# Weight pairs converted as one 512-wide tile, three step tables in place of two, in a fused attention and mixture-of-experts kernel

## The chip, the cores and the metric

The kernel runs on one core of a Trainium2 chip. The metric is the device time of one execution in microseconds (us), from the kernel's start to its end; lower is better. The profiled execution is one more execution, seen by the hardware profiler. Engines are named as the profile names them: PE is TensorE (PEld its weight loads), DVE is VectorE, ACT is ScalarE, POOL is GpSimd, SP is SyncE, whose queue issues most of the DMAs.

## The reference

Three layers follow one another. The two weight matrices of the middle layer arrive as 64-bit floats; everything else is 32-bit.

```
# 1: attention, 4 batches x 8 heads, 576 positions, 64 wide, top 32 of each row
scores = scale * q @ k.T
kth = np.partition(scores, -32, axis=-1)[..., -32:-31]
scores = np.where(scores >= kth, scores, -1e9)
x = softmax(scores) @ v                       # -> 2304 tokens x 512

# 2: dense layer, w_in 512 x 2048 and w_out 2048 x 512 (float64)
h = x @ w_in
x = (h * np.clip(h + 3.0, 0.0, 6.0) / 6.0) @ w_out

# 3: one of 8 experts for each token
logits = normed(x) @ normed(expert_emb).T / tau
e = argmax(logits);  gate = softmax(logits)[e]
out[token] = gate * (relu(x[token] @ w1[e]) @ w2[e])
```

## The kernel before, in words

**Units and steps.** The attention is cut into 72 units; a unit is 128 query rows of two heads. The kernel walks through 76 steps of a software pipeline. In step `i` the scores of unit `i` are computed, the top 32 of unit `i-1` are picked, unit `i-2` is masked, unit `i-3` goes through the exponential and is scaled, and unit `i-4` is transposed and multiplied by V. The picking is done on DVE: `pairs` (lines 409 to 413) sorts the 576 scores of each row into two halves, and `select` (lines 428 and 431, called `pick0` to `pick3`) takes eight maxima at a time. Line 411 runs once for each unit, so the distance between two of its rows is the length of a step.

**The dense layer beside it.** From step 12 on, each step also works on one of 72 items of the dense layer (nine groups of 256 tokens, eight slices of the hidden width each): `s10` and `s11` are the first product on PE (line 568), `gate` and `large` are ACT's, `swish` is DVE's, `small` is POOL's, and `s20` and `s21` are the second product (line 603) for the item of the step before. The steps in `PAUSE` take no item. A finished group is written to `y_dram` (`out_y`) and its tokens are scored against the experts (`route`, then `choose`, `rank` and `place`, taken one at a time by `aside`).

**The weights.** In the first steps the float64 weights are converted, in 32 pairs of pieces, each piece 128 x 256. `w_load` brings the two words of each number, one piece a tile. DVE shifts the exponent and the upper mantissa bits of the high word into place with two operations per piece, both reading two tiles in SBUF (`w_one`, line 234, and `w_two`, line 238). The 29 low bits are then treated in one of two ways: three pieces of four are rounded on ACT (`w_round`, line 246) and added on POOL (`w_add`, line 251), one of four is merged by a third DVE operation (line 241). The result is split into a high part on ACT (`w_hi`, line 259) and a low part on POOL (`w_low`, line 263), and the low part is stored to DRAM (`w_store`). Steps 0 to 4 convert one pair each (`RAMP`), steps 5 to 18 up to two.

**The order.** Inside the loop the order of instructions is written out by hand: the strings `FIRST` (steps 0 to 20, `WORDS`) and `THEN` list the parts of a step, and every engine and every DMA queue takes its instructions in that order.

**The end.** After the loop a scheduler orders the code by priorities. The last group of the dense layer (tokens of groups 16 and 17) is a special case before: its second product, the routing of its tokens (`finals`), the first half-layer of expert 0 (`stage1(0, ...)`) and the splitting of that expert's weights are interleaved by hand (lines 992 to 1026), and the weights of the second expert are asked for ahead of them. Then the eight experts follow.

Of the kernel before, what the change touches and what calls it, by code (L numbers as in the profile page):

```python
# [54 lines left out]
def fused_kernel(tc: tile.TileContext, *args):  # L55
# [35 lines left out]
def layers(tc: tile.TileContext, qt, kt, v, w_in, w_out, embt, tau, w1, w2, out, y_dram, g_dram, x_dram, tbl, lo_dram, flag, pools, consts):  # L91
# [4 lines left out]
    m1, sm, fs, ps_a = pools[1:]  # L96
# [26 lines left out]
    stg = st.enter_context(tc.tile_pool(name="stg", bufs=5))  # L123
# [24 lines left out]
    def embed(part):  # L148
# [6 lines left out]
        elif part == 1:  # L155
            onesf = mp.tile([128, 128], F32, tag="ug", name="onesf", bufs=1)
            nc.vector.memset(onesf, 1.0)
            sq = fs.tile([128, 4, E], F32, tag="gts", name="sq")
            nc.vector.tensor_tensor(sq, emb["et"], emb["et"], op=ALU.mult)
# [3 lines left out]
        elif part == 2:  # L163
# [30 lines left out]
    wpieces = []  # L194
    for q in range(8):
        c = slice(256 * q, 256 * q + 256)
        for k in range(4):
            wpieces.append((w_in[128 * k:128 * k + 128, c], (vh[:, k - k % 2:k - k % 2 + 2, c], lo_dram[0][q][:, 256 * (k - k % 2):256 * (k - k % 2) + 512])))
        for k in range(2):
            for c in (slice(0, 256), slice(256, 512)):  # L200
                wpieces.append((w_out[128 * (2 * q + k):128 * (2 * q + k) + 128, c], (wh[:, 2 * q + k, :], lo_dram[1][q][:, 512 * k:512 * k + 512])))
    ent_ = {}
    cnt, stored = [0], [0]
# [23 lines left out]
    def w_one(n):  # L227
        e = ent_[n]
        e["both"] = mp.tile([128, DM], F32, tag="wf", name="wf", bufs=3)
        for o, (raw, single, _) in enumerate(e["raws"]):  # L230
            if single:
                nc.vector.tensor_copy(e["both"][:, 256 * o:256 * o + 256], raw)
# [937 lines left out]
```

## Time and profile before

| | us |
|---|---|
| median of three runs | 1165.76 |
| lowest and highest of them | 1165.2 and 1168.55 |
| the profiled execution, its own time | 1164.9 |
| its span, first to last instruction | 1163.2 |
| busy: PE, DVE, ACT, POOL | 1008.5, 818.5, 732.6, 646.4 |
| end of the conversion, start of line 411 in unit 18 | 241.9 |

The busy figures are for the whole span. Over the first 240 us DVE is busy nearly all the time and PE about half of it or less; from there on PE is busy nearly all the time. So the two stretches are read apart. An engine's rows overlap slightly (an instruction's row starts about 0.08 us before the one ahead of it on DVE has ended), so a sum over a step is taken from start to start.

### The profile page before, as it was taken

The numbers are of one execution on the slowest core, as the hardware profiler recorded it, in microseconds if no ns is written. First come the engines' busy times: TensorE is split into PE (matmuls) and PEld (weight loads), VectorE is DVE, ScalarE is ACT, GpSimd is POOL, SyncE is SP. The second block draws the span as 40 slices with busy tenths as digits, with TensorE's granted clock in tenths as the row PEclk, the third lists the DMA queues.
The fourth block names the chain that finished last, engine by engine and source line by source line (L and its number), as shares of the span: only waits on it lengthen the run. The fifth ranks groups of instructions, "written<-read, shape, count | busy, mean of one in ns | idle before, by whom it ended". The sixth has DMA issues, their size and how long they took to land. (4 is left out here: it accounts for less than half of the span.)

```text
span 1163.2 us, 21146 instructions
## 1 busy us (share of the span) xinstructions
PE 1008.5 (87%) x7200; PEld 892.1 (77%) x7200; DVE 818.5 (70%) x2429; ACT 732.6 (63%) x1486; POOL 646.4 (56%) x833
## 2 busy tenths in 40 slices
PE   2455576789999979999979998999989999999994
PEld 1344465679998869998868997889978788888884
DVE  4999999999788968788968789922142534444440
ACT  4676776878778868778868778743334444444540
POOL 5676776777666867666867666653231442213210
PEclk9966577889999989999989999999999999999998
DMA  6444455665443446443446244356765463344440
GB/s 179 146 137 138 164 167 174 185 199 204 123 123 116 134 144 194 123 123 118 136 121 213 82 146 128 110 128 177 235 214 208 117 221 122 128 175 148 173 175 20
DMA packets 93014, 176.45 MB, mean 152 GB/s; under 512 B 21135, under 2 KB 38690, under 8 KB 92895
## 3 DMA queue, kind: packets, MB, share of 16 engines
q1 hardware_dynamic: 88255, 164.90, 45.2%
q0 software_dynamic: 4640, 10.10, 2.6%
q8 instruction: 59, 0.97, 0.4%
q14 instruction: 60, 0.49, 0.1%
HBM read 151.15 MB, written 19.71 MB: 147 GB/s over the span
## 5 line engine op out<-in xcount | busy, mean ns | idle before, releaser
L446 POOL TENSOR_TENSOR s<-s,z 128x576 f32<-128x576 f32 x144 | 189.8, 1323 | 70.2 <-ACT z L442 69.5
L568 PE MATMUL bank_h<-xh,vh 128*128 128x256 f32 x576 | 177.0, 307 | 0.8 <-DVE u L580 0.8
L568 PE MATMUL bank_h<-xh,lo 128*128 128x256 f32 x576 | 167.7, 291 | 3.7 <-DMA lo<-lo_dram 3.7
L568 PE MATMUL bank_h<-xl,vh 128*128 128x256 f32 x576 | 167.7, 291 | 2.8 <-DVE xl L524 2.8
L428 DVE MAX8 A<-left 128x8 f32<-128x288 f32 (+1 forms) x288 | 159.7, 595 | 0.0
L397 PE MATMUL ps_sc<-kst,qh 128*128 128x288 f32 x256 | 90.8, 367 | 71.6 <-DVE left L413 35.9
L587 POOL TENSOR_TENSOR gl<-u,gh 128x512 fp32r<-128x512 f32 x72 | 93.2, 1295 | 102.8 <-ACT gh L584 88.8
L484 ACT COPY pt<-bank_t 128x384 f32<-128x384 f32 x216 | 100.4, 475 | 59.1 <-PE bank_t L479 58.9
L479 PE MATMUL bank_t<-ident,s 128*128 128x128 f32 x648 | 108.2, 294 | 28.0 <-ACT pt L484 16.7
L397 PEld LDWEIGHTS ps_sc<-kst,qh 128*128 128x128 f32 x256 | 55.7, 218 | 88.4 <-issue 73.6
L400 ACT COPY s<-ps_sc 128x576 f32<-128x576 f32 x144 | 91.5, 635 | 41.8 <-PE ps_sc L397 38.4
L568 PEld LDWEIGHTS bank_h<-xh,lo 128*128 128x128 f32 x576 | 114.2, 198 | 4.3 <-DMA lo<-lo_dram 4.3
L568 PEld LDWEIGHTS bank_h<-xl,vh 128*128 128x128 f32 x576 | 114.3, 198 | 3.6 <-DVE xl L524 3.1
L580 DVE SCALAR_TENSOR_TENSOR u<-u,bank_h 128x512 f32<-128x512 f32 x72 | 49.2, 684 | 95.6 <-ACT u L576 95.3
L603 PE MATMUL y<-wh,gh 128*128 128x512 f32 x288 | 116.3, 404 | 0.0
L807 DVE TENSOR_TENSOR l<-a,h 128x1024 fp32r<-128x1024 f32 x64 | 78.0, 1243 | 54.2 <-ACT h L806 51.5
L479 PEld LDWEIGHTS bank_t<-ident,s 128*128 128x128 f32 x648 | 82.3, 150 | 44.0 <-ACT pt L484 20.1
L568 PEld LDWEIGHTS bank_h<-xh,vh 128*128 128x128 f32 x576 | 114.2, 198 | 1.6 <-DVE u L580 1.0
L603 PE MATMUL y<-wh,gl 128*128 128x512 f32 x288 | 113.0, 397 | 2.0 <-POOL gl L587 2.0
L603 PE MATMUL y<-lo,gh 128*128 128x512 f32 x288 | 113.9, 396 | 0.2 <-DMA lo<-lo_dram 0.2
L442 ACT ACTIVATE z<-s,nb 128x576 bf16<-128x576 f32 x144 | 111.7, 780 | 0.8 <-POOL nb L436 0.7
L452 ACT ACTIVATE s<-s,nb 128x576 f32<-128x576 f32 x144 | 112.1, 778 | 0.0
(240 smaller groups left out, 2778.9 us busy)
## 6 DMA issues: line engine op xcount, KB each, us to landing
lo<-lo_dram SPq DMA_DIRECT2D x144, 512.0 KB, 4.2
a<-in_moe_w_dram SPq DMA_DIRECT2D x64, 512.0 KB, 7.4
qraw<-in_q_dram SPq DMA_DIRECT2D x64, 128.0 KB, 3.0
w<-in_moe_w_in_dram SPq DMA_DIRECT2D x32, 256.0 KB, 3.4
lo_dram<-wf SPq DMA_DIRECT2D x32, 256.0 KB, 2.4
w<-in_moe_w_out_dram SPq DMA_DIRECT2D x32, 256.0 KB, 3.0
vt<-in_v_dram SPq DMA_DIRECT2D x16, 320.0 KB, 4.5
kraw<-in_k_dram SPq DMA_DIRECT2D x32, 144.0 KB, 4.3
```

The source lines that it names most:

```text
L397: nc.tensor.matmul(ps[:, n, :HS], t, kk[:, HS * g:HS * g + HS], start=(o == 0), stop=(o == len(parts) - 1))
L400: nc.scalar.copy(sbuf[i % NS][:, :, HS * g:HS * g + HS], ps_[i][:, :, :HS])
L428: nc.vector.max(A[:, n, 8 * r:8 * r + 8], src[:, n, :w])
L442: nc.scalar.activation(zb_[n], tile_of(i, n), AF.Relu, bias=sel[i][1][:, n, 1:2], scale=-BIG)
L446: nc.gpsimd.tensor_tensor(s, s, zb_[n], op=ALU.subtract)
L452: nc.scalar.activation(s, s, AF.Exp, bias=sel[i][1][:, n, 0:1], scale=SCALE, accum_out=sums[i][:, n:n + 1])
L479: nc.tensor.transpose(pp[:, 128 * k:128 * k + 128], e[:, 128 * (3 * c + k):128 * (3 * c + k) + 128], ident)
L484: nc.scalar.copy(pts[i][:, 3 * c:3 * c + 3, :].rearrange("p k n -> p (k n)"), tb_.pop((i, c))[:, :384])
L568: nc.tensor.matmul(ph[:, a, :], w, x[:, k, :], start=(k == 0 and n == 0), stop=(k == 3 and n == 2))
L587: nc.gpsimd.tensor_tensor(state[q][1], state.pop((q, "u")).rearrange("p (a n) -> p a n", a=2), state[q][0].bitcast(F32), op=ALU.subtract)
L603: nc.tensor.matmul(state["y"][o], x[:, a, c], w, start=(f == 0 and n == 0), stop=(f == 15 and n == 2))
L807: nc.vector.tensor_tensor(lo, x, hi.bitcast(F32), op=ALU.subtract)
```

## The change

Conversion: a pair is loaded by one DMA into one tile of 512 numbers, three such tiles in place of five of 256. The first bit operation becomes a `tensor_scalar` (one tile and two constants), the second stays a `scalar_tensor_tensor`; both work on 512 numbers at once. Every pair is rounded on ACT and added on POOL; the third DVE operation is no longer reached. The tables: `FIRST` now holds for steps 0 to 11, the new `MID` for steps 12 to 20, and `THEN` has another order. The preparation of the expert embedding is cut into five parts and its square moves to ACT. At the end, the special case for the last group is gone: the last group goes through the same loop as the others, and the weights of the second expert are asked for later.

```diff
-RAMP, WORDS = 5, 21
-FIRST = ("turn0 lows ship hi0 expo0 low0 hi1 s10 keep0 load_k expo1 turn1 bend0 one0 guard pick0 store0 score0 low1 two0 mask0 pick1 "
-         "turn2 inverse s11 pick2 round1 bend1 keep1 take0 keep2 load_q mask1 s20 score1 round0 gate one1 scale two1 values swish "
-         "take1 large aside add0 store1 pick3 pairs load0 add1 xh load1 s21 small bounds xl prep need_v")
-THEN = ("pick0 turn0 turn1 expo0 keep0 s10 expo1 lows ship turn2 pick1 pick2 s11 keep1 keep2 guard bend0 score0 gate take0 load_k "
-        "values mask0 score1 inverse swish scale pick3 bend1 xh load_q take1 prep need_v mask1 bounds aside large s20 xl pairs "
-        "s21 small place")
+RAMP, MOES, WORDS = 5, 12, 21
+FIRST = ("hi0 turn0 bend0 keep0 turn1 pick0 lows ship turn2 bend1 keep1 keep2 expo0 expo1 pick1 one0 round1 s10 hi1 s20 s21 score0 "
+         "low0 load_k values take0 load_q two0 mask0 guard round0 inverse s11 store0 pick2 pick3 mask1 gate aside low1 xh score1 "
+         "scale swish take1 large prep one1 two1 add0 bounds small add1 xl load0 load1 pairs store1 need_v")
+MID = ("lows s10 round0 expo0 hi0 turn0 turn1 one0 expo1 s11 gate two0 s20 pick0 low0 pick1 guard s21 bend0 ship keep0 score0 "
+       "load_k store0 keep1 turn2 add0 hi1 swish one1 take0 mask0 keep2 load_q inverse score1 large values round1 two1 take1 "
+       "pick2 aside bend1 load0 scale xh pick3 low1 small add1 mask1 need_v pairs xl prep load1 store1 bounds")
+THEN = ("lows turn0 pick0 expo0 keep0 turn1 expo1 s10 s11 ship bend0 turn2 score0 keep1 pick1 guard gate take0 keep2 inverse "
+        "mask0 swish scale large aside bend1 pick2 load_k s20 pick3 score1 take1 s21 values small prep mask1 pairs place xh "
+        "bounds load_q xl need_v")
@@
-    stg = st.enter_context(tc.tile_pool(name="stg", bufs=5))
+    stg = st.enter_context(tc.tile_pool(name="stg", bufs=3))
@@ def embed(part):
-            sq = fs.tile([128, 4, E], F32, tag="gts", name="sq")
-            nc.vector.tensor_tensor(sq, emb["et"], emb["et"], op=ALU.mult)
+            emb["sq"] = fs.tile([128, 4, E], F32, tag="gts", name="sq")
+            nc.scalar.activation(emb["sq"], emb["et"], AF.Square)
+        elif part == 2:
+            onesf, sq = emb["ones"], emb["sq"]
@@ def w_one(n):
-            nc.vector.scalar_tensor_tensor(t, raw[:, :, 1], 3, raw[:, :, 1], op0=ALU.logical_shift_left, op1=ALU.bitwise_xor)
+        nc.vector.tensor_scalar(t, raw[:, :, 1], 3, 0x3FFFFFFF, op0=ALU.logical_shift_left, op1=ALU.bitwise_and)
@@ def w_two(n):
-            nc.vector.scalar_tensor_tensor(t, t, 0x3FFFFFFF, raw[:, :, 1], op0=ALU.bitwise_and, op1=ALU.bitwise_xor)
-            if not rounded:
-                nc.vector.scalar_tensor_tensor(t, raw[:, :, 0], 29, t, op0=ALU.logical_shift_right, op1=ALU.bitwise_or)
+        nc.vector.scalar_tensor_tensor(t, raw[:, :, 1], -0x40000000, t, op0=ALU.bitwise_and, op1=ALU.bitwise_or)
@@ def w_load(n):
-                raw = stg.tile([128, 256, 2], I32, tag="st", name="w64")
+            raw = stg.tile([128, 512, 2], I32, tag="st", name="w64")
-            raws.append((raw, single, cnt[0] % 4 != 3))
+        ent_[n] = dict(dst=dst, raw=raw, single=single, rounded=True)
@@ def out_y(o):
-            final = gs[o] >= NG - 2
-            if final:
-                finals.append((t, gs[o]))
-            else:
-                route(t, gs[o])
+            route(t, gs[o])
@@
-        while moe or side:
+        while moe or last or side:
@@
-        with tc.manual_schedule():
-            for o in range(2):
-                last[6](last[0], o)
...
-            load1(1)
...
-            stage1(0, 0, 256, (4,))
-            split2(0, range(5, 8), lambda f: stage1(0, 0, 256, (f,)))
+        with tc.high_priority(offset=500):
+            stage1(0, 0, 256)
+        split2(0)
@@
-                if r:
-                    load1(then)
+                load1(then)
                 load2(then)
```

## Rows read from the trace of the kernel before

**Rows 1.** Busy time in three stretches; columns: stretch, length, PE, PEld, DVE, ACT, POOL, PEclk.

```profile
81.60:94.30 12.70, 7.14 (x37) 5.67 (x37) 12.67 (x38) 9.12 (x21) 9.26 (x12) 0.50 0.40 137
158.20:241.90 83.70, 59.32 (x412) 51.85 (x413) 81.84 (x221) 63.59 (x134) 60.70 (x71) 0.81 0.59 183
241.90:745.00 503.10, 480.85 (x3938) 432.89 (x3937) 430.92 (x1503) 392.46 (x846) 358.93 (x503) 0.97 0.46 140
```

**Rows 2.** Timeline of DVE, line 411, units 0, 4, 11 and 18.

```profile
16.54 0.75 DVE L411 TENSOR_TENSOR left<-ps_sc,s 128x576 f32<-128x576 f32 x1
...
57.37 0.75 DVE L411 TENSOR_TENSOR left<-ps_sc,s 128x576 f32<-128x576 f32 x1
...
144.90 0.75 DVE L411 TENSOR_TENSOR left<-ps_sc,s 128x576 f32<-128x576 f32 x1
...
241.89 0.75 DVE L411 TENSOR_TENSOR left<-ps_sc,s 128x576 f32<-128x576 f32 x1
```

**Rows 3.** Timeline of DVE in one step, its conversions and what follows them.

```profile
88.13 0.51 DVE L428 MAX8 A<-top 128x8 f32<-128x144 f32 x2
...
90.74 0.75 DVE L234 SCALAR_TENSOR_TENSOR wf<-w 128x256 int32<-128x256 int32 x2
91.41 0.75 DVE L238 SCALAR_TENSOR_TENSOR wf<-wf,w 128x256 int32<-128x256 int32 x2
92.08 1.41 DVE L428 MAX8 A<-left 128x8 f32<-128x576 f32 x2
...
95.85 0.75 DVE L234 SCALAR_TENSOR_TENSOR wf<-w 128x256 int32<-128x256 int32 x2
96.52 0.51 DVE L428 MAX8 A<-top 128x8 f32<-128x144 f32 x2
...
97.50 1.94 DVE L238 SCALAR_TENSOR_TENSOR wf<-wf,w 128x256 int32<-128x256 int32 x2
99.36 1.50 DVE L241 SCALAR_TENSOR_TENSOR wf<-w,wf 128x256 int32<-128x256 int32 x1
100.79 0.51 DVE L428 MAX8 A<-top 128x8 f32<-128x144 f32 x2
```

**Rows 4.** Timeline of POOL at the same time; brackets: idle before, and its releaser.

```profile
91.96 1.49 POOL L251 TENSOR_TENSOR wf<-wf,w 128x256 int32<-128x256 int32 x2 [3.15 <-issue]
...
93.87 0.73 POOL L381 TENSOR_TENSOR ql<-qraw,qh 128x256 fp32r<-128x256 f32 x1
94.56 1.27 POOL L263 TENSOR_TENSOR wf<-wf,vh 128x512 fp32r<-128x512 f32 x1
...
97.70 2.88 POOL L446 TENSOR_TENSOR s<-s,z 128x576 f32<-128x576 f32 x2
```

**Rows 5.** Groups over the whole span: count | busy us, mean ns of one | idle before.

```profile
L580 DVE SCALAR_TENSOR_TENSOR u<-u,bank_h 128x512 f32<-128x512 f32 x72 | 49.2, 684 | 95.6 <-ACT u L576 95.3
L246 ACT ACTIVATE w<-w 128x256 int32<-128x256 uint32 x48 | 19.7, 442 | 1.8 <-DMA w<-in_moe_w_in_dram 1.7
```

**Rows 6.** Waits of PE, 158 to 242 us: total, times, longest.

```profile
PE bank_a L162 <- DVE sq L159: 9.3, 1, 9.3
```

**Rows 7.** Waits of PE, 242 to 745 us: total, times, longest.

```profile
PE bank_t L479 <- ACT pt L484: 14.5, 11, 2.9
```

**Rows 8.** Timeline of ACT near 410 us, where a new batch's keys arrive.

```profile
410.00 0.67 ACT L322 CAST kst<-kraw 128x576 fp32r<-128x576 f32 x1 [2.51 <-DMA kraw<-in_k_dram]
```

**Rows 9.** Timeline of PE and POOL around the end of the dense layer.

```profile
886.13 0.39 PE L603 MATMUL y<-wh,gl 128*128 128x512 f32 x1
887.20 0.66 PE L1008 MATMUL pxt<-ident,ysl 128*128 128x128 f32 x4 [0.68 <-ACT ysl L614]
...
899.42 0.98 POOL L699 DMA_INDIRECT tbl<-ids,rows  x1 [0.30 <-issue]
```

**Rows 10.** Busy time by stretch around and after it; columns as in rows 1.

```profile
886.00:915.00 29.00, 25.26 (x172) 22.34 (x171) 13.31 (x51) 13.83 (x26) 5.92 (x8) 0.97 0.54 154
915.00:1130.00 215.00, 211.72 (x1229) 185.20 (x1228) 101.83 (x133) 98.99 (x153) 60.52 (x59) 1.00 0.46 162
```

More of the change, by code (lines that the diff above doesn't have):

```diff
@@ L209, in w_load @@
     def w_load(n):
-        raws = []
-        for src, dst in (wpieces[2 * n], wpieces[2 * n + 1]):
-            single = src.dtype == F32
-            if single:
-                raw = stg.tile([128, 256], F32, tag="st", name="w32")
-                nc.sync.dma_start(out=raw, in_=src)
-            else:
-                raw = stg.tile([128, 256, 2], I32, tag="st", name="w64")
-                nc.sync.dma_start(out=raw, in_=src.bitcast(I32).rearrange("p (n two) -> p n two", two=2))
-                cnt[0] += 1
-            raws.append((raw, single, cnt[0] % 4 != 3))
@@ L221, in w_load @@
-        ent_[n] = dict(dst=wpieces[2 * n][1], raws=raws)
-    def words_of(e):
-        return [(raw, e["both"][:, 256 * o:256 * o + 256].bitcast(I32), rounded)
-                for o, (raw, single, rounded) in enumerate(e["raws"]) if not single]
+        src, dst = wpairs[n]
+        single = src.dtype == F32
+        if single:
+            raw = stg.tile([128, 2, 256], F32, tag="st", name="w32")
+            nc.sync.dma_start(out=raw, in_=src)
+        else:
+            raw = stg.tile([128, 512, 2], I32, tag="st", name="w64")
+            nc.sync.dma_start(out=raw.rearrange("p (a n) two -> p a n two", a=2), in_=src.bitcast(I32).rearrange("p a (n two) -> p a n two", two=2))
@@ L243, in w_round @@
     def w_round(n):
-        for raw, single, rounded in ent_[n]["raws"]:
-            if rounded and not single:
-                nc.scalar.activation(raw[:, :, 0], raw[:, :, 0].bitcast(U32), AF.Copy, scale=2.0 ** -29)
+        e = ent_[n]
+        if e["rounded"] and not e["single"]:
+            raw = e["raw"]
+            nc.scalar.activation(raw[:, :, 0], raw[:, :, 0].bitcast(U32), AF.Copy, scale=2.0 ** -29)
     def w_add(n):
-        for raw, t, rounded in words_of(ent_[n]):
-            if rounded:
-                nc.gpsimd.tensor_tensor(t, t, raw[:, :, 0], op=ALU.add)
+        e = ent_[n]
@@ L253, in parts_of @@
+        if e["rounded"] and not e["single"]:
+            nc.gpsimd.tensor_tensor(e["words"], e["words"], e["raw"][:, :, 0], op=ALU.add)
     def parts_of(e):
@@ L779, in finish_counts, with load_ids @@
             nc.vector.tensor_copy(flag[:, 1:2], vf)
-    def expert(r):
+    def load_ids(r, b0, b1):
         if r not in evs:
@@ L844, in ahead @@
         load2(0)
-        expert(1)
     def step(i, last):
@@ L939, in layers, with split2 @@
                 finish_rest()
-        assert "w1" in late and done_groups[0] == NG - 2
+        if "w1" not in late:
+            at.close()
+            ahead()
+        assert done_groups[0] == NG and "order" in late
+        st.close()
+        hp = mb.enter_context(tc.tile_pool(name="hp", bufs=1))
+        tk = mb.enter_context(tc.tile_pool(name="tk", bufs=1))
+        wb = mb.enter_context(tc.tile_pool(name="wb", bufs=1))
+        gp = mb.enter_context(tc.tile_pool(name="gp", bufs=3))
+        px = mb.enter_context(tc.tile_pool(name="px", bufs=2, space=PSUM))
+        po_ = mb.enter_context(tc.tile_pool(name="po_", bufs=3, space=PSUM))
         hs = {}
-        def split2(r, then=(), f=None):
-            then = deque(then)
+        def split2(r):
             a2 = ws2[r]
@@ L948, in split2, with stage1 @@
                 split(h2[:, k:k + 2, :], l2[:, k:k + 2, :], a2[:, k:k + 2, :])
-                if then:
-                    f(then.popleft())
             ws2[r] = (h2, l2)
-        def stage1(r, c0, c1, fs_=range(8)):
+        def stage1(r, c0, c1):
             xh_, xl_ = tok[r]
@@ L958, in stage1 @@
             hh, hl = hs[r]
-            for f in fs_:
+            for f in range(8):
                 ph = late["ph"].tile([128, 512], F32, tag="ph", name="ph2")[:, :c1 - c0]
```

84 lines of the change are left out of this document (27 added, 57 removed).

## The prediction

> **What bounds the kernel now.** I read busy time by stretch first, then the length of a step from line 411, then DVE and POOL side by side within one step, and last the waits of PE.
>
> In the early stretch DVE is busy for 12.67 of 12.70 us, ACT for 9.12, POOL for 9.26 and PE for 7.14 [rows 1]. DVE sets the step there. From 241.9 us on it is PE, busy for 480.9 of 503.1 us [rows 1], and so it stays through the experts, 211.7 of 215 us [rows 10]. What PE has to do after 241.9 us is nearly the same work in both kernels, so a microsecond won before that point should arrive at the end undiminished, as long as nothing behind it grows.
>
> Line 411 stands at 16.54, 57.37, 144.90 and 241.89 us for units 0, 4, 11 and 18 [rows 2]. The steps between are thus 40.83/4 = 10.21 us with one pair, 87.53/7 = 12.50 us with two pairs, and 96.99/7 = 13.86 us with two pairs and, mostly, an item of the dense layer beside them.
>
> Now the inside of a step of 12.66 us, 88.13 to 100.79 [rows 3]. The conversions take 90.74 to 92.08 (four operations, 1.34 us), 95.85 to 96.52 (two, 0.67 us) and 97.50 to 100.79 (three, 3.29 us): 5.30 us. What remains, the selection and small things, is 7.36 us. Undisturbed, one operation takes 1.34/4 = 0.335 us from start to start, so nine would take 3.02 us. The other 2.28 us are lost in the last group: the second operation there and the one behind it, each reading two tiles in SBUF, are held while POOL runs its two L446 back to back from 97.70 to 100.58 [rows 3, 4]. So DVE is not only full, it is also standing in line behind POOL.
>
> **The conversion.** *DVE.* Nine operations on 256 numbers become four on 512. The nearest row for one on 512 is L580, 684 ns [rows 5]; with the 0.08 us overlap between neighbours that is 0.60 us from start to start. Four cost 2.40 us, and DVE's own work in a step goes from 7.36 + 3.02 = 10.38 to 9.76 us. The first operation is now a `tensor_scalar`, which the trace does not show on such tiles. I bound it by 0.335 us (the price of half the numbers) and 0.60 us, and take 0.60, because L580 has the same shape; at the lower end DVE's work is 9.23 us.
>
> By the Trainium skill (VectorE: DVE Perf Modes, section "The perf-mode tier table") a 32-bit `tensor_scalar` from SBUF to SBUF runs at twice the rate of a two-tensor operation, which would put the price near the lower end. No row here shows such an operation.
>
> *POOL.* Two adds of 256 numbers take 1.49 us, so 0.745 each; from 256 to 512 numbers POOL's subtractions go from 0.73 to 1.27 us [rows 4], so an add of 512 costs about 0.745 x 1.27/0.73 = 1.30 us. Three adds in a step (0.745 x 2 + about 0.9 for one that is held) become two, 2.6 in place of 2.4 us: POOL goes from 9.26 to about 9.45 us. *ACT.* Three roundings at 0.44 us [rows 5] become two of twice the size, between 0.44 and 0.88 us each, so ACT moves by -0.4 to +0.4 us from 9.12: no bound.
>
> *Who stands in line now.* If DVE's second operations and POOL's work exclude each other, as the held pair shows, the two need 9.45 + 2 x 0.60 = 10.65 us a step. DVE alone needs 9.76, which leaves 0.9 us for waits. I take **10.6 us**. The lower end is 9.76 us, no wait at all; it would need POOL to be idle just then, as it is today before the first adds (3.15 us, [rows 4]). The upper end is that both second operations wait as long as the two held ones do today, 2.28 us together: 12.04 us.
>
> Stretch by stretch. Units 4 to 11: 7 x (12.50 - 10.6) = **13.3 us** (3.2 to 19.2). Units 11 to 18: today they stand 1.36 us above the others; I leave that, since the dense layer's ACT, DVE and POOL work is the same, so 11.96 us, 7 x 1.9 = **13.3 us** (3.2 to 22.8). The upper end there holds one thing more: PE waits 9.3 us for the square of the expert embedding, which sits at the end of a DVE step [rows 6], and the change moves it to ACT and puts a step between. Units 0 to 4: one pair costs 1.2 in place of 1.5 us and there is half the waiting; but new keys are cast on ACT there too. From 10.21 to 9.5 us: **2.8 us** (0 to 4.8). Together 29.4 us.
>
> *Fewer tiles, larger loads.* With three tiles for two pairs in work, the first load of the next step finds a free tile, the second waits until POOL has added the first pair, and on SP the store of the low part and the next `ship` stand behind it. In my reading of the new tables that add ends about 2 us ahead of the step's end and the second pair is wanted 4 to 5 us into the next step. I cost it at nothing; the cover is those 6 us, and if a load took longer, DVE would wait for the difference, once a step.
>
> **The order in `THEN`.** Of the 22.2 us for which PE is idle from 241.9 to 745 us, 14.5 us are 11 waits of transposes for ACT's copy `keep` [rows 7], the longest where a batch's new keys are late and hold ACT for 2.51 us [rows 8]. The new table puts `s11` between the second and the third transpose, which gives ACT the time of 12 matmuls more; for that `xh` becomes one of ACT's last and waits for `values`, now last on PE. Bounds: a gain of 14.5 us, and a loss of as much. I take a gain of **4 us**: the cover is PE work that was there already, and half of the waits are short.
>
> **The end.** Before, PE's last matmul of the dense layer ends at 886.52 us and the last entry of the routing at 900.40 us, 13.9 us later [rows 9]; PE fills that time with `stage1` of expert 0 and is idle for 29.00 - 25.26 = 3.7 us up to 915 us [rows 10]. After, the same `stage1` is there to be run, it needs nothing of the routing, but the order is the scheduler's; one buffer for the transposed tokens in place of two adds a copy to the chain; the second expert's weights are asked for later, though PE still has two stages of expert 0 ahead of them. Bounds: a gain of 3.7 us (no idle time left), a loss of 13.9 - 3.7 = 10.2 us (PE idle all along). I take a loss of **2 us**, near today's row, because the work that fills the gap is independent.
>
> **Sum.** 29.4 + 4 - 2 = 31.4 us. The profiled execution has 1164.9 us, 1.7 us more than its span; 1164.9 - 31.4 = 1133.5. The median of the runs shown is 0.9 us above that execution, so 1134 us.
>
> **The rivals.** *The line moves with the work* (1156 us). Both second operations are held as long as two are today: steps of 12.04 and 13.4 us. For it: POOL is busier than before and has fewer pauses to slip into. Against it: four chances to be held where there were nine. It leaves 3.2 + 3.2 + 1.0 us of the gain, and with the other two terms 1165.8 - 9.4.
>
> *All four are held* (1183 us, slower). If the `tensor_scalar` also needs what POOL holds, DVE's work is 9.23 us at the lower price, but each of four operations may wait 1.14 us: 13.79 us against 12.50, 1.29 us more in 14 steps, about 0.4 in the first four, 19.5 us in all, less the 2 us of the other terms. It decides from 0.82 us a wait on ((12.50 - 9.23)/4). For it: the back-to-back pattern of the held pair, where POOL's next instruction gets in between two of DVE's. Against it: the six operations before them in the same step are not held at all, since POOL waits just then for their result. The Trainium skill (SBUF — State Buffer, section "Who interferes with whom") says that a `tensor_scalar` in its two-port mode contends with GpSimd and that the loser is blocked for the whole instruction; the held pair agrees for two inputs, for a `tensor_scalar` no row here shows it.
>
> *The routing is exposed* (1143 us). PE idles through the 13.9 us: 10.2 in place of 2 us.
>
> *`THEN` eats it* (1165 us, no change). If the new place of `xh` costs PE half a microsecond in each of 53 steps, 26 us and the 4 us are gone. Against it: ACT is busy for 392 of 503 us there [rows 1], so it has 2 us a step to spare.
>
> *No waiting at all* (1115 us): the lower ends, 9.76 us and its like.
>
> **Chances.** The forecast 0.55 (its own range 1122 to 1148), the line that moves 0.17, the exposed routing 0.10, all four held 0.08, no waiting 0.06, `THEN` 0.04. The range of 1122 to 1157 us leaves out the slower rival, most of the best case, and a little of the others, about 2 in 10. A difference of about 0.3%, 3.5 us, is what a measurement of this kernel can tell from none. Faster by more: 0.55 + 0.17 + 0.10 + 0.06, less 0.02 for the far end of the second, 0.86. Within: 0.05. Slower: 0.09.
>
> **What would show it.** Line 411 of units 4 and 11 lie 74 us apart, and unit 18 comes at about 212 us. The rows of the first operation last about as long alone as beside POOL if it isn't held; the second ones spread up to 1.3 us longer. PE's waits for `keep` between there and the last unit come to well under 14 us, and around the end of the dense layer PE is idle for under 8 us. The forecast is wrong if the steps stay above 12 us, if DVE waits for a load once a step, or if unit 18 comes early and the end does not.

## The result, and the profile after

The changed kernel takes 1124.91 us, the median of 4 runs (1123.61 to 1126.44), against 1165.80 us before: a ratio of 0.9645, with a 95% interval of 0.9625 to 0.9666. The profiled execution has a span of 1123.8 us, against 1163.2. Lines of the changed kernel lie one further down in the step loop, so L412 here is L411 of [rows 2].

First the length of a step: timeline of DVE, line 412, units 0, 4, 11 and 18 (start and duration in us).

```profile
17.42 0.75 DVE L412 TENSOR_TENSOR left<-ps_sc,s 128x576 f32<-128x576 f32 x1
...
53.58 0.75 DVE L412 TENSOR_TENSOR left<-ps_sc,s 128x576 f32<-128x576 f32 x1
...
124.72 0.75 DVE L412 TENSOR_TENSOR left<-ps_sc,s 128x576 f32<-128x576 f32 x1
...
217.57 0.75 DVE L412 TENSOR_TENSOR left<-ps_sc,s 128x576 f32<-128x576 f32 x1
```

Set against [rows 2] and unit 70, the last but one (the same line at 737.88 us before and at 693.41 after), this says where the 39.4 us of span were won:

| stretch | before, us | after, us | gain | forecast |
|---|---|---|---|---|
| start to unit 0 | 16.5 | 17.4 | -0.9 | 0 |
| units 0 to 4 | 40.8 | 36.2 | 4.7 | 2.8 |
| units 4 to 11 | 87.5 | 71.1 | 16.4 | 13.3 |
| units 11 to 18 | 97.0 | 92.9 | 4.1 | 13.3 |
| units 18 to 70 (`THEN`) | 496.0 | 475.8 | 20.2 | 4 |
| unit 70 to the end | 425.3 | 430.4 | -5.1 | -2 |

The time came out below the forecast by 9 us, mainly because one term was far too small (by 16 us) and two were too large (by 9 and 3 us). Busy time of the last four stretches (length, then PE, PEld, DVE, ACT, POOL, and the granted clock):

```profile
53.60:124.70 71.10, 44.30 (x277) 35.48 (x278) 70.38 (x218) 65.43 (x137) 63.72 (x69) 0.71 0.53 173
124.70:217.60 92.90, 65.89 (x481) 56.28 (x480) 77.70 (x222) 72.28 (x146) 72.94 (x76) 0.85 0.60 185
217.60:693.40 475.80, 465.16 (x3877) 414.07 (x3877) 422.99 (x1478) 385.00 (x835) 357.68 (x501) 1.00 0.47 148
693.40:1110.00 416.60, 398.01 (x2499) 351.10 (x2495) 167.18 (x318) 174.98 (x297) 122.64 (x128) 0.99 0.49 160
```

In the first stretch DVE is still what bounds, busy for 70.38 of 71.10 us. In the second nothing is full: DVE is idle for 15 of 92.9 us, so something else holds the engines there (the waits below show what). In the third PE is busy for 465.2 us at full clock, where the same 52 steps before took it 473.7 us at 0.97 (row under e1 and e2 below).

**Inside a step, units 4 to 11.** Timeline of DVE: the first conversion of the run, then one step of 10.28 us, its conversions and what stands next to them:

```profile
15.32 0.43 DVE L232 TENSOR_SCALAR wf<-w 128x512 int32<-128x512 int32 x1 [14.38 <-DMA w<-in_moe_w_in_dram]
...
93.89 0.75 DVE L412 TENSOR_TENSOR left<-ps_sc,s 128x576 f32<-128x576 f32 x1
...
97.23 0.56 DVE L232 TENSOR_SCALAR wf<-w 128x512 int32<-128x512 int32 x1
97.83 0.69 DVE L239 SCALAR_TENSOR_TENSOR wf<-w,wf 128x512 int32<-128x512 int32 x1
98.44 0.16 DVE L460 RECIPROCAL sums<-sums 128x2 f32<-128x2 f32 x1
...
101.41 1.03 DVE L232 TENSOR_SCALAR wf<-w 128x512 int32<-128x512 int32 x1
102.47 0.72 DVE L239 SCALAR_TENSOR_TENSOR wf<-w,wf 128x512 int32<-128x512 int32 x1
103.11 0.28 DVE L525 TENSOR_TENSOR xl<-bank_a,xh 128x128 fp32r<-128x128 f32 x1
...
104.17 0.75 DVE L412 TENSOR_TENSOR left<-ps_sc,s 128x576 f32<-128x576 f32 x1
```

POOL at the same time:

```profile
96.22 1.29 POOL L447 TENSOR_TENSOR s<-s,z 128x576 f32<-128x576 f32 x1
97.60 0.27 POOL L457 TENSOR_SCALAR sums<-sums 128x2 f32<-128x2 f32 x1
97.95 1.73 POOL L447 TENSOR_TENSOR s<-s,z 128x576 f32<-128x576 f32 x1
99.63 1.27 POOL L264 TENSOR_TENSOR wf<-wf,vh 128x512 fp32r<-128x512 f32 x1
100.87 1.28 POOL L252 TENSOR_TENSOR wf<-wf,w 128x512 int32<-128x512 int32 x1
```

The conversions take 97.23 to 98.44 and 101.41 to 103.11, 2.91 us in place of the 5.30 us read from [rows 3]; what remains of the step is 7.37 us, as before. The `tensor_scalar` L232 ends 0.28 us after POOL's first L447 (97.51 to 97.79) and, in its second row, 0.29 us after POOL's L252 (102.15 to 102.44). Where POOL runs nothing beside it, it takes 0.43 us (the row at 15.32; 0.42 from here on). So it is held beside POOL both times. The two-tensor operation L239 comes straight behind it and is not held; there it is POOL that waits: the L447 that starts 0.12 us into L239 takes 1.73 us in place of 1.29. The other steps of units 4 to 11 look the same: of their 14 rows of L232, 12 take 0.50 to 1.05 us, and all 14 of L239 take 0.69 to 0.72. In units 11 to 18 L239 is held too, in 6 of 13 rows, with 1.64 to 1.65 us.

**Units 11 to 18.** The step from 150.4 to 167.1 us takes 16.7 us. Waits of all engines from 136 to 168 us (total, times, longest):

```profile
ACT u L577 <- PE bank_h L569: 9.6, 1, 9.6
...
PE bank_a L167 <- DVE xl L525: 7.9, 1, 7.9
POOL s L447 <- ACT z L443: 6.9, 1, 6.9
DVE u L581 <- ACT u L577: 5.6, 1, 5.6
```

The DVE operation that PE waits for:

```profile
151.75 0.28 DVE L525 TENSOR_TENSOR xl<-bank_a,xh 128x128 fp32r<-128x128 f32 x1
```

And PE:

```profile
152.18 1.85 PE L167 MATMUL bank_a<-sq,onesf 128*128 128x8 f32 x8 [7.93 <-DVE xl L525]
...
154.24 0.41 PE L569 MATMUL bank_h<-xl,vh 128*128 128x256 f32 x1
...
159.04 0.28 PE L569 MATMUL bank_h<-xh,vh 128*128 128x256 f32 x1
```

L167 is the expert embedding's sum of squares. It stands in PE's queue, wants a half of `bank_a`, and starts 0.15 us after DVE's `xl`, a reader of `bank_a`, has ended. Everything behind it on PE waits too: the products L569 come late, ACT's `gate` waits for them 9.6 us, and instructions of DVE and POOL wait for ACT. The granted clock falls to half at 148.6 us, 4 us into PE's pause, and comes back at 158.9: the first L569 behind the pause take 0.41 us each, the later ones 0.28.

**The waits of units 18 to 70** that the prediction named, PE from 217.6 to 701 us:

```profile
PE bank_t L480 <- ACT pt L485: 4.3, 7, 0.7
```

That was 14.5 us in 11 waits, the longest 2.9 [rows 7].

### The profile page after: what moved, and what is told of

Same layout as the page of the kernel before. It is cut to its first block, busy times and chain, and to the rows that moved or that the text cites. A ratio compares the mean times of both kernels' runs of the same rounds, so it can differ in the third digit from the quotient of the medians.

```text
span 1123.8 us, 20871 instructions
## 1 busy us (share of the span) xinstructions
PE 991.6 (88%) x7200; PEld 870.5 (77%) x7200; DVE 776.2 (69%) x2347; ACT 729.7 (65%) x1471; POOL 651.0 (58%) x818
## 4 chain that ended last, share of the span: by engine, by line
PE 59%; DVE 14%; DMA 11%; issue 8%; ACT 4%; POOL 2%; SPq 1%; POOLq 0%; DVEq 0%; ACTq 0%
PE bank_h L569 16%; PE y L604 15%; PE bank_a L498 6%; PE ph L965 5%; PE ps_sc L398 5%; PE bank_t L480 5%; DMA out_dram<-ob,idt 4%; PE po L978 4%; DVE A L429 4%; DVE left L432 2%; DVE wf L239 2%; DVE wf L232 1%; PE bank_t L641 1%; DMA lo<-lo_dram 1%; DMA lo_dram<-wf 1%
## 5 line engine op out<-in xcount | busy, mean ns | idle before, releaser
L447 POOL TENSOR_TENSOR s<-s,z 128x576 f32<-128x576 f32 x144 | 189.1, 1313 | 33.3 <-ACT z L443 31.9
L569 PE MATMUL bank_h<-xh,vh 128*128 128x256 f32 x576 | 170.7, 296 | 1.1 <-DVE u L581 1.1
L569 PE MATMUL bank_h<-xl,vh 128*128 128x256 f32 x576 | 164.6, 286 | 1.6 <-DVE xl L525 1.6
L569 PE MATMUL bank_h<-xh,lo 128*128 128x256 f32 x576 | 164.3, 285 | 0.2 <-DMA lo<-lo_dram 0.2
L480 PE MATMUL bank_t<-ident,s 128*128 128x128 f32 x648 | 104.9, 290 | 36.9 <-ACT pt L485 28.6
L398 PE MATMUL ps_sc<-kst,qh 128*128 128x288 f32 x256 | 87.1, 353 | 49.4 <-DVE left L414 23.5
L799 DVE TENSOR_TENSOR l<-a,h 128x1024 fp32r<-128x1024 f32 x64 | 78.0, 1246 | 62.9 <-ACT h L798 62.9
L480 PEld LDWEIGHTS bank_t<-ident,s 128*128 128x128 f32 x648 | 73.8, 145 | 54.6 <-ACT pt L485 34.7
L569 PEld LDWEIGHTS bank_h<-xh,vh 128*128 128x128 f32 x576 | 112.0, 194 | 2.8 <-DVE u L581 1.3
L569 PEld LDWEIGHTS bank_h<-xl,vh 128*128 128x128 f32 x576 | 112.1, 195 | 2.2 <-DVE xl L525 1.8
L569 PEld LDWEIGHTS bank_h<-xh,lo 128*128 128x128 f32 x576 | 111.9, 194 | 0.7 <-DMA lo<-lo_dram 0.7
L498 PE MATMUL bank_a<-pt,vt 128*64 128x128 f32 (+1 forms) x1600 | 103.9, 282 | 0.7 <-DVE pos L679 0.7
L498 PEld LDWEIGHTS bank_a<-pt,vt 128*64 128x64 f32 x1600 | 86.4, 147 | 22.9 <-issue 7.6
```

What stands on the lines that cost most here:

```text
L398: nc.tensor.matmul(ps[:, n, :HS], t, kk[:, HS * g:HS * g + HS], start=(o == 0), stop=(o == len(parts) - 1))
L447: nc.gpsimd.tensor_tensor(s, s, zb_[n], op=ALU.subtract)
L480: nc.tensor.transpose(pp[:, 128 * k:128 * k + 128], e[:, 128 * (3 * c + k):128 * (3 * c + k) + 128], ident)
L498: nc.tensor.matmul(av[64 * n:64 * n + 64, c0:c1], vt[:, k, 64 * n:64 * n + 64], pt[:, k + 5 * n if k < 4 else 4, c0:c1], start=(o == 0), s ...
L569: nc.tensor.matmul(ph[:, a, :], w, x[:, k, :], start=(k == 0 and n == 0), stop=(k == 3 and n == 2))
L799: nc.vector.tensor_tensor(lo, x, hi.bitcast(F32), op=ALU.subtract)
```

## The experiments

The twelve kernels ran in three groups, each on one chip; the kernel before ran beside each group, with medians of 1171.35 (e1 to e4), 1170.45 (e5 to e8) and 1167.25 us (e9 to e12). Ratios are to those, with 95% intervals. Stretches are from each kernel's profile, by the rows that answer to [rows 2]. A profile is one execution, and can lie some us from its kernel's median: e1's is 5.6 us below, e10's and e11's 2.7 and 4.2 us above.

| kernel | ratio | 4 to 11 | 11 to 18 | unit 18 at | 18 to 70 | 70 to end |
|---|---|---|---|---|---|---|
| before | 1 | 87.5 | 97.0 | 241.9 | 496.0 | 425.3 |
| changed (first chip) | 0.9645 | 71.1 | 92.9 | 217.6 | 475.8 | 430.4 |
| e1 only the new `THEN` | 0.9867 (0.9820 to 0.9914) | 87.5 | 97.0 | 242.1 | 477.7 | 428.6 |
| e2 all but the new `THEN` | 0.9860 (0.9819 to 0.9902) | 71.3 | 91.4 | 215.5 | 496.0 | 439.0 |
| e3 all but the new end | 0.9598 (0.9558 to 0.9639) | 71.1 | 93.1 | 217.8 | 476.3 | 426.3 |
| e4 embedding 6 steps earlier | 0.9597 (0.9556 to 0.9638) | 76.7 | 83.9 | 213.5 | 476.1 | 433.7 |
| e5 only the conversion | 0.9728 (0.9678 to 0.9778) | 74.7 | 85.4 | 213.0 | 496.9 | 428.8 |
| e6 only the early tables | 0.9966 (0.9935 to 0.9998) | 88.5 | 98.1 | 242.6 | 495.0 | 427.7 |
| e7 bits by two-tensor operations | 0.9741 (0.9702 to 0.9780) | 74.8 | 95.9 | 226.1 | 474.8 | 442.6 |
| e8 `FIRST` in place of `MID` | 0.9715 (0.9676 to 0.9754) | 71.3 | 94.2 | 218.1 | 483.6 | 433.8 |
| e9 changed, once more | 0.9656 (0.9625 to 0.9687) | 71.3 | 94.0 | 218.5 | 475.7 | 429.2 |
| e10 old end, embedding's matmuls moved | 0.9559 (0.9529 to 0.9589) | 71.3 | 87.4 | 212.2 | 476.7 | 428.6 |
| e11 old end, old `FIRST` for `MID` | 0.9542 (0.9512 to 0.9571) | 71.1 | 83.7 | 208.8 | 478.0 | 429.6 |
| e12 both | 0.9541 (0.9511 to 0.9572) | 71.3 | 83.1 | 209.3 | 478.5 | 425.5 |

### What `THEN` is worth: e1 and e2

e1 is the kernel before with nothing but the new `THEN`; e2 is the changed kernel with the old one.

```diff
-THEN = ("pick0 turn0 turn1 expo0 keep0 s10 expo1 lows ship turn2 ... s21 small place")
+THEN = ("lows turn0 pick0 expo0 keep0 turn1 expo1 s10 s11 ship bend0 turn2 ... xl need_v")
```

> The kernel before with the new order of THEN and nothing else. In the two traces the stretch from unit 18 to unit 70 went from 496.0 to 475.8 us: PE's idle time there from 22.0 to 10.5 us, and PE's busy time by 8.7 us, with a granted clock of 1.00 in place of 0.97. Theory A: all of that is the order in THEN. Then this kernel takes 20 us less than before, about 1146, and its early stretch (unit 18 at 242 us) stays. Theory B: the order is worth the 4 us of the forecast, and the rest comes from the new early stretch, which hands PE over at another clock: then about 1162.

Measured: 1155.66 us, 15.7 below the kernel before on that chip; units 18 to 70 in 477.7 us, 18.3 less, with 3.3 us lost behind them.

> The changed kernel with the old order of THEN. Theory A (the order is worth 20 us): about 1145, with PE waits for the copy of the transposes back at about 14 us. Theory B (worth 4 us): about 1129.

Measured: 1156.34 us; units 18 to 70 in 496.0 us, as in the kernel before. The string alone makes 18 to 20 us in this stretch, with the old conversion as well as with the new. (e2 as a whole lies further above the changed kernel, since its end is 8.5 us longer; see the section on the end.) Busy time from unit 18 to 70 of the kernel before, of e1 and of e2:

```profile
241.89:737.88 495.99, 473.74 (x3876) 426.35 (x3875) 425.03 (x1480) 388.15 (x837) 356.07 (x500) 0.97 0.46 141
```

```profile
242.10:719.77 477.67, 464.28 (x3868) 413.26 (x3870) 423.18 (x1479) 384.18 (x834) 357.94 (x500) 1.00 0.47 146
```

```profile
215.53:711.53 496.00, 472.30 (x3880) 424.92 (x3879) 425.11 (x1479) 388.73 (x838) 356.30 (x501) 0.98 0.46 142
```

With the old string PE is idle for 22 to 24 us, with the new one for 11 to 13. It is also busy 7 to 9 us longer for nearly the same number of matmuls, at a clock of 0.97 or 0.98. In the kernel before, the stretches at half clock come to 26.4 us of these 496.0: 5.9 us are left over from the early steps (up to 247.8 us), 20.5 us stand near pauses (10.2 around 410 to 432 us, 10.2 around 585 to 606 us). In e1 and in the changed kernel there are none. Here they are in the kernel before, around the wait of 2.9 us that [rows 7] gives as the longest:

```profile
400.00:411.60 11.60, 9.12 (x80) 7.86 (x78) 11.43 (x39) 8.66 (x19) 7.33 (x13) 1.00 0.68 183
411.60:418.40 6.80, 5.45 (x29) 5.17 (x31) 4.62 (x20) 5.16 (x12) 6.17 (x7) 0.50 0.10 20
418.40:428.70 10.30, 7.69 (x60) 6.77 (x57) 6.93 (x26) 5.87 (x15) 5.26 (x7) 1.00 0.63 193
428.70:432.10 3.40, 3.40 (x24) 3.12 (x24) 0.91 (x3) 2.76 (x5) 3.20 (x5) 0.50 0.04 7
```

```profile
412.95 0.90 PE L479 MATMUL bank_t<-ident,s 128*128 128x128 f32 x3 [2.86 <-ACT pt L484]
...
414.08 0.41 PE L568 MATMUL bank_h<-xh,lo 128*128 128x256 f32 x1
```

PE was idle for 2.5 us of the 11.6 before 411.6 and did not start again until 412.95; the clock fell to half (1.2 GHz) at 411.6, within that pause, and L568 then took 0.41 us a matmul in place of 0.28. So this wait was paid twice: as idle time, and in the matmuls after it.

The other kept profiles agree on the busy time: in units 18 to 70 PE is busy for 464 to 465 us in the seven kernels with the new string and at most 0.9 us at half clock, 466.7 in e11 and e12 (new string, 3.4 us), 468.3 in e8 (new string, 6.8 us), 471.8 in e5 and 472.3 in e2 (old string, 13.7 and 20.5 us), and 473.7 before (26.4 us). The length does not follow it one for one, as e5 shows (the new conversion with the old string, below):

```profile
213.00:709.88 496.88, 471.83 (x3885) 424.48 (x3886) 425.10 (x1479) 388.81 (x839) 357.01 (x501) 0.99 0.46 141
```

It has half the time at half clock of the kernel before and is busy 1.9 us less, but it is idle 2.8 us more and takes as long. Fewer microseconds at half clock did not by themselves shorten the stretch here.

### Conversion or tables: e5 and e6

e5 puts the new conversion (and the embedding in five parts) under the old tables and the old end; e6 puts the new `FIRST` and `MID` over the old conversion, with the old `THEN` and the old end.

```diff
 # e5: conversion as changed
-        for name in (FIRST if i < MOES else MID if i < WORDS else THEN).split():
+        for name in (FIRST if i < WORDS else THEN).split():   # FIRST, THEN and end as before
```

> The kernel before with the new conversion (512-wide pairs, two operations, all rounded on ACT and added on POOL, three tiles, the embedding in five parts) under the old tables FIRST and THEN and the old end. To be read up to unit 18. Theory A: the conversion itself brings the gain, since DVE's work of a step falls from 10.4 to about 9.2 us: units 4 to 11 in 71 to 75 us, against 87.5 before and 71.1 after. Theory B: the gain needs the new tables, since the old ones put the longer operations where POOL holds them: above 78 us.

Measured: 1139.96 us; unit 18 at 213.0 us, 28.9 earlier than before, and so 4.6 us earlier than in the changed kernel.

```diff
 # e6: conversion as before
-        for name in (FIRST if i < WORDS else THEN).split():
+        for name in (FIRST if i < MOES else MID if i < WORDS else THEN).split():   # THEN and end as before
```

> The kernel before with the new FIRST and MID but the old conversion, the old THEN and the old end. To be read up to unit 18. Theory A (the conversion brings the gain): units 4 to 11 stay within 2 us of 87.5, as DVE still has nine operations a step. Theory B (the order brings it, by keeping DVE's operations out of POOL's way): the 2.3 us of holding in a step go, and the stretch takes about 73 us.

Measured: 1167.21 us, 0.3% below the kernel before; unit 18 at 242.6 us. Busy time from unit 4 to 11, of e5 and of e6:

```profile
52.97:127.63 74.66, 47.61 (x274) 38.98 (x274) 74.18 (x219) 65.18 (x136) 64.61 (x70) 0.68 0.53 171
```

```profile
56.00:144.53 88.53, 49.82 (x274) 38.12 (x275) 86.22 (x254) 63.63 (x140) 68.21 (x76) 0.64 0.45 139
```

The gain before unit 18 is the conversion's. The new `FIRST` gives 3.5 us more on top of it (74.7 to 71.1) and nothing without it. `MID` takes more than that back: units 11 to 18 need 85.4 us under the old table and 92.9 under the new one. What in `MID` does it, the section on the stall shows.

### The price of the `tensor_scalar`: e7

```diff
-        nc.vector.tensor_scalar(t, raw[:, :, 1], 3, 0x3FFFFFFF, op0=ALU.logical_shift_left, op1=ALU.bitwise_and)
+        nc.vector.scalar_tensor_tensor(t, raw[:, :, 1], 3, raw[:, :, 1], op0=ALU.logical_shift_left, op1=ALU.bitwise_xor)
...
-        nc.vector.scalar_tensor_tensor(t, raw[:, :, 1], -0x40000000, t, op0=ALU.bitwise_and, op1=ALU.bitwise_or)
+        nc.vector.scalar_tensor_tensor(t, t, 0x3FFFFFFF, raw[:, :, 1], op0=ALU.bitwise_and, op1=ALU.bitwise_xor)
```

> The changed kernel with the first bit operation as a scalar_tensor_tensor that reads the tile twice, and the second to match, as before the change but 512 wide. In the changed kernel the tensor_scalar on 512 numbers takes 0.42 us where POOL doesn't hold it, and a two-input operation 0.69 us. Theory A (DVE and its line behind POOL set the step): 0.27 us more for each pair, so units 4 to 11 go from 71.1 to about 75, units 0 to 4 by 1 us, 11 to 18 by 2 to 4 us, in all about 7 us slower than the changed kernel. Theory B (ACT, busy for 65.4 of 71.1 us there, or POOL sets the step): within 1 us of the changed kernel.

Measured: 1141.71 us; 74.8 us for units 4 to 11 against 71.1. Timeline of DVE in e7, the first conversion of the run and the second pair of a step:

```profile
16.00 0.69 DVE L232 SCALAR_TENSOR_TENSOR wf<-w 128x512 int32<-128x512 int32 x1 [15.06 <-DMA w<-in_moe_w_in_dram]
...
84.00 1.28 DVE L232 SCALAR_TENSOR_TENSOR wf<-w 128x512 int32<-128x512 int32 x1
85.32 0.72 DVE L239 SCALAR_TENSOR_TENSOR wf<-wf,w 128x512 int32<-128x512 int32 x1
```

The first operation takes 0.69 us alone, 0.27 more than the `tensor_scalar`, and 1.28 us where it is held, 0.25 more than the held one of the changed kernel. Over the 14 rows of units 4 to 11 the mean of L232 goes from 0.74 to 1.00 us, and that of L239 stays. Two a step over 7 steps make 2 x 0.26 x 7 = 3.6 us, and the stretch grew by 3.6. That confirms DVE, with what it waits for, as the bound there, and 0.42 us as the term that was set at 0.60 + 0.08. The end of e7 is 12 us longer than that of the changed kernel, though its code there is the same; the section on the end below comes back to it.

### The stall in units 11 to 18: e4, e8, e10, e11, e12

e4 moves the embedding's five parts to steps 5 to 10; e8 uses the new `FIRST` through step 20.

```diff
-        if i in (11, 12, 13, 14, 16):
-            embed((11, 12, 13, 14, 16).index(i))
+        if i in (5, 6, 7, 8, 10):
+            embed((5, 6, 7, 8, 10).index(i))
```

> The changed kernel with the five parts of the expert embedding's preparation at steps 5, 6, 7, 8 and 10 in place of 11, 12, 13, 14 and 16; the work is the same. Theory A: the 16.7 us between units 13 and 14 are the matmuls of that preparation, which stand in PE's queue ahead of the dense layer's first product and wait 7.9 us for something late in DVE's step; at steps where PE has no dense work they are hidden: unit 18 about 7 us earlier, about 1118 in all. Theory B: the new table MID makes ACT wait for that product in any case, and the stall moves to another step: about 1125.

Measured: 1125.21 us. Units 11 to 18 fall from 92.9 to 83.9 us, units 4 to 11 rise from 71.1 to 76.7: most of the stall moved with the embedding. Unit 18 is 4 us earlier, the end 3.2 us longer. So with the embedding out of its steps `MID` needs no more time (83.9 us) than the old order does in e11 below (83.7): what costs the 9 us is the embedding's place in `MID`, not the rest of that order.

```diff
-RAMP, MOES, WORDS = 5, 12, 21
+RAMP, MOES, WORDS = 5, 21, 21
```

> The changed kernel with the table FIRST for steps 0 to 20, so without MID. In MID the gate of the dense layer stands ahead of most of ACT's work, so ACT waits for the first product (9.6 us in one step). Theory A: MID is what holds units 11 to 18 at 92.8 us where the forecast had 84; with FIRST they take 84 to 88 us. Theory B: FIRST asks for the first product of the dense layer in the middle of the step and starves PE at its low clock: over 95 us, and MID is worth what it costs.

Measured: 1138.03 us; 94.2 us for units 11 to 18, no better than `MID`, and units 18 to 70 7.7 us longer; the two steps from unit 18 on, still under `FIRST`, take 28.8 us in place of 18.8. Beside items of the dense layer the new `FIRST` is thus no gain; which of its places costs that was not tried.

The last four share a chip. e9 is the changed kernel itself.

> The changed kernel once more, beside the next three on the same chip, so that they can be set against it. Both theories: units 11 to 18 in about 93 us, from unit 70 to the end about 430 us.

Measured: 1127.08 us, a ratio of 0.9656: what the next three are held against.

e10 has the old end (as e3 below) and issues the embedding's matmuls ahead of `score0` in step 14, the other parts where they were:

```diff
+            if name == "score0" and i == 14:
+                embed(2)
```

> The changed kernel with the old end, and with the matmuls of the embedding's preparation moved from the end of step 13 to the middle of step 14, ahead of the scores, where the value that they wait for is long there. Theory A (the 7.9 us wait is theirs, and the end costs 4 to 5 us): units 11 to 18 in about 86 us in place of 93, the end in about 426 us, together 11 to 12 us less than the changed kernel. Theory B (MID holds ACT behind the dense layer's first product in any case): units 11 to 18 at 90 us or more, 4 to 5 us less in all.

Measured: 1116.57 us, 10.5 below e9. The step with the stall goes from 17.1 to 11.1 us, and units 11 to 18 from 94.0 to 87.4, not to 83.7: part of the wait is left. The wait of PE that was 7.9 us, in e10 from 124.75 to 212.19 us:

```profile
PE bank_a L167 <- DVE xl L525: 3.7, 1, 3.7
```

e11 has the old end and the old `FIRST`'s string as `MID`:

```diff
-MID = ("lows s10 round0 expo0 hi0 turn0 ... pairs xl prep load1 store1 bounds")
+MID = ("turn0 lows ship hi0 expo0 low0 ... add1 xh load1 s21 small bounds xl prep need_v")
```

> The changed kernel with the old end and, for steps 12 to 20, the old table FIRST in place of MID. With that table throughout, the new conversion took 85.4 us for units 11 to 18, against 92.8 with MID. Theory A (MID itself is the worse order there): about 85 us, with the end 12 us less than the changed kernel. Theory B (the 85.4 us came from the state that the slower steps before had left, fewer steps ahead of PE): over 90 us.

Measured: 1114.03 us, 13.1 below e9. Busy time from unit 11 to 18 in e11:

```profile
125.09:208.82 83.73, 60.40 (x472) 51.98 (x470) 80.27 (x222) 74.51 (x149) 72.95 (x76) 0.88 0.65 202
```

Here DVE is busy for 80.3 of 83.7 us, so it bounds again, and the stretch comes out at the length forecast for it. Both reforms together, e12:

> As the one before (old end, old FIRST for steps 12 to 20), with the embedding's matmuls in the middle of step 14. Theory A (their wait stalls PE in this table too, as it did for 9.3 us before the change): units 11 to 18 in about 80 us and the whole 4 to 6 us below the one before. Theory B (in this table DVE sets those steps and PE's wait is hidden): no difference over 1 us.

Measured: 1114.50 us, the same as e11. The wait is down to 0.9 us (fence below, e12 from 126 to 210 us), but units 11 to 18 gain only 0.6 us by it: with the old order the 3.3 us that PE waits in e11 were beside DVE's work.

```profile
PE bank_a L167 <- DVE xl L525: 0.9, 1, 0.9
```

e11 and e12 are the fastest kernels here, at 0.954 of the kernel before, and below the changed kernel by an interval that does not touch its own.

### The end: e3

```diff
-            route(t, gs[o])
+            if final:
+                finals.append((t, gs[o]))
+            else:
+                route(t, gs[o])
...
-        with tc.high_priority(offset=500):
-            stage1(0, 0, 256)
-        split2(0)
+        with tc.manual_schedule():
+            ...   # the last routing, stage1 and split2 in the old order by hand
```

> The changed kernel with the special case for the last group put back (its second product, its routing, expert 0's first stage and the early request of the second expert's weights, ordered by hand). From the last unit's selection to the end the traces have 414.2 us before and 419.5 after. Theory A: the removed special case costs those 5.3 us, mostly as PE's two waits for gathered tokens (5.0 and 2.8 us, at 873 and 877 us) and the lower clock right after them: about 1119. Theory B: the end is as good as before, and the 5 us come from elsewhere, as from a different state of the loop's last steps: about 1125.

Measured: 1125.69 us, a ratio of 0.9598; its interval overlaps that of the changed kernel, so the timing doesn't separate the two. Nor do the lengths in their profiles, 426.3 against 430.4 us from unit 70: e1, e3, e10, e11 and e12 run the same order of matmuls behind unit 70 and take 425.5 to 429.6 us, and e9, with the changed kernel's end, takes 429.2. What does differ is how long PE waits for gathered tokens around there: 8.5 to 10.2 us in the six profiles with the new end, 1.8 to 6.2 in the eight with the old one. Apart from the last 13 us, e3 has no time at half clock behind unit 70 and the changed kernel 10.2 us; but e10 and e11, with the old end, have 10.2 and 6.8 us. POOL around the routing, first in the changed kernel, then in e3:

```profile
855.72 2.25 POOL L669 TENSOR_TENSOR before<-before,picks 128x8 bf16<-128x8 bf16 x2 [16.27 <-DVE picks L667]
860.93 1.01 POOL L694 DMA_INDIRECT tbl<-ids,rows  x1 [2.96 <-DVE df L1005]
862.24 0.98 POOL L694 DMA_INDIRECT tbl<-ids,rows  x1 [0.30 <-issue]
```

```profile
851.34 0.47 POOL L675 TENSOR_TENSOR before<-before,picks 128x8 bf16<-128x8 bf16 x2 [11.33 <-DVE picks L673]
854.83 1.00 POOL L700 DMA_INDIRECT tbl<-ids,rows  x1 [3.02 <-DVE df L1039]
856.13 0.98 POOL L700 DMA_INDIRECT tbl<-ids,rows  x1 [0.30 <-issue]
```

PE in the changed kernel, the last matmul of the dense layer and the waits for the gathered tokens:

```profile
843.77 0.40 PE L604 MATMUL y<-wh,gl 128*128 128x512 f32 x1
...
873.26 1.11 PE L818 MATMUL pxt<-ident,xg 128*128 128x128 f32 x4 [5.04 <-DMA xg<-y_dram,idt]
877.12 0.58 PE L818 MATMUL pxt<-ident,xg 96*128 96x96 f32 x2 [2.75 <-DMA xg<-y_dram,idt]
```

From the dense layer's last matmul (844.17) to the last routing entry (863.22) it is 19.1 us, against 13.9 us in [rows 9]. PE does not idle there, but when the tokens of expert 0 that need the routing are wanted, they come 5.04 and 2.75 us late, and PE goes on at half clock for a while (872.3 to 882.5 us). Ends that the scheduler orders took 429.2 to 442.6 us in six profiles, those by hand 425.3 to 429.6 in eight. The two longest of the former are e7's 442.6 and e2's 439.0: there PE's order among the experts' matmuls differs from that of the changed kernel, although neither edits the end. That the new end costs about 4 us is therefore likely, from the waits and from all the profiles together, but no pair of runs shows its size.

## Why the prediction was right, and where not

**What bounds the early steps, and that a microsecond won there arrives:** right. DVE is busy for 70.38 of 71.10 us after the change. In e5, which has the old order and the old end behind unit 18, that unit comes 28.9 us earlier and the whole kernel takes 30.5 us less than the kernel before beside it.

**The price of four operations, 10.6 us a step:** right in size, 10.16 on average, but not by the mechanism named. The 10.6 us rested on the second operations standing in line behind POOL; in units 4 to 11 none of them does (0.69 to 0.72 us in 14 rows), and the `tensor_scalar` does. Two errors partly cancel. The `tensor_scalar` was taken at 0.60 us from start to start, as [rows 5] has it for the same shape; it is 0.34 us, the lower bound (0.42 us less the overlap). Alone, the four take 2 x (0.34 + 0.61) = 1.9 us. In the step shown they take 2.91, so the line behind POOL costs 1.0 us, small gaps included, where 0.9 had been set aside. The Trainium skill (VectorE: DVE Perf Modes, section "The perf-mode tier table") gives a `tensor_scalar` on fp32 in SBUF twice the rate of a `tensor_tensor`. That pointed the right way for int32 too, against the row that was chosen: 0.42 us here, against 0.69 for the `scalar_tensor_tensor` on as many numbers.

**The rival in which all four are held:** its condition is true, its price is not. The `tensor_scalar` does wait for POOL, twice in the step shown. But it takes 0.14 and 0.61 us more, and the operations behind it 0 and 0.03: 0.78 us in all, where 4 x 0.82 were needed to lose. The row of [rows 3] on which the 1.14 us rested was a place where POOL had two long instructions back to back. The Trainium skill (SBUF — State Buffer, section "Who interferes with whom") says that a `tensor_scalar` in its two-port mode contends with GpSimd; the two rows that end 0.28 and 0.29 us after POOL's agree.

**Units 11 to 18, 83.7 us:** wrong by 9 us, and not through the conversion, whose e5 takes 85.4 us there under the old table. The step that failed is "I leave that, since the dense layer's ACT, DVE and POOL work is the same": it priced work and not order. The new `MID` sends the embedding's matmuls into PE's queue some 8 us before `xl`, a reader of `bank_a`, has ended, and PE, ACT, POOL and DVE stand still in turn. The prediction had seen the wait of 9.3 us in [rows 6] and put it down to the square. Moving the square to ACT left the wait as it was (7.9 us), now released by `xl`; e10 moves the matmuls and has the old end, which lies far behind: that step takes 6 us less. With the embedding out of `MID` (e4) the stretch is 83.9 us, with the old order in its place (e11) 83.7, as forecast. That the matmuls wait for `xl`, the profile says, and the wait shrinks when they move (3.7 us in e10, 0.9 in e12). That they do so because both use `bank_a` is read from the names; no run gives them another bank.

**`THEN`, 4 us:** right in kind, wrong in size by 16 us. The waits for `keep` went from 14.5 to 4.3 us, 10 us where 4 were counted ("half of the waits are short"); that lay within the bounds of 14.5. All of PE's idle time fell by 11.6 us. What lay outside the bounds is PE's busy time: 8.6 us less for nearly the same matmuls (473.74 to 465.16, e1: 464.28), with the 26.4 us at half clock gone. The step that failed is the bound: it was made from idle time alone, and the term for matmuls at half clock was missing from it. The two parts are not independent: e5 has less time at half clock than the kernel before and more idle time, at the same length. How much of the gain would remain if the pauses stayed and the clock didn't fall no run here can tell.

**The end, -2 us:** -5.1 between these two profiles, within the bounds, where ends of the same order of matmuls differ by up to 4 us. "One buffer for the transposed tokens in place of two adds a copy to the chain" fits what happened: the second group's copy (ACT L635) starts 4.2 us behind the first's, in place of 1.8, an operation that splits weights (DVE L799, 1.23 us) gets in ahead of `picks`, which ends 11.5 us after the dense layer in place of 8, and L669 is then held beside more such splits, 2.25 us in place of 0.47. Whether the one buffer or the scheduler's order put the copy there was not tried. The place was wrong: PE idles when the tokens are wanted, 24 us on, and loses some of the clock there too.

**Larger loads at nothing:** nearly. Unit 0 comes 0.9 us later, and over the first 18 units DVE waits 7.5 us ahead of L232, 5.2 of it for the store of a low part that still holds a `wf` buffer; in units 4 to 11 all its idle time is 0.7 us. The load of the second pair is not in these waits.

That the sum came out near is in part luck: the term that was too small (16 us) and those that were too large (9 and 3 us) were of opposite signs. The forecast's 74 us for units 4 to 11 were 71.1, unit 18 came at 217.6 in place of 212, and the end was late.

## What to carry to other kernels

A pause of PE can cost more than its length, where matmuls run at half clock behind it, so a bound made from idle time alone can be too small: compare PE's busy time and granted clock for the same number of matmuls. A reordered step is to be priced by who stands first in each in-order queue and what it waits for: here eight small matmuls in the wrong place held up four engines. Test the parts of a change apart; of this one, the conversion and the new `THEN` carry the gain, the embedding's place in `MID` gave some of it back, and the new end probably did.

## What the runs showed of the hardware

- A `tensor_scalar` with two bit operations on int32 takes 0.42 us on 512 numbers, as a two-tensor operation takes on 256 (0.41); one of the latter on 512 takes 0.69. It is held by POOL all the same: 0.56 and 1.03 us beside L447 and L252.
- In these rows the one that starts later is held, and it goes both ways: POOL's L447 took 1.73 us in place of 1.29, started 0.12 us into L239, and its two small adds 2.25 in place of 0.47, started 0.17 us into DVE's splits; the two held rows of L232 started 1.01 us into an L447 and 0.54 us into L252.
- The granted clock fell to half (1.2 GHz) 1.5 us into a pause of PE of 2.86 us, at the end of 11.6 us in which PE was busy for 9.12; it stayed there for 6.8 us, with 256-column matmuls at 0.41 in place of 0.28 us. It also fell at 428.7 us, where PE was busy throughout the next 3.4 us. At the end of the changed kernel it fell 4.1 us into a pause of 5.04 us and stayed at half for 10.2 us, which hold another pause of 2.75 us.
